# New priorities and engine homes in the list schedule of an attention and two expert layers

## The chip, the cores and the metric

The kernel runs on one core of one Trainium2 chip. The core has a matrix engine (TensorE, PE in the profile, with its weight loads as PEld), a vector engine (VectorE, DVE), a scalar engine (ScalarE, ACT), a general engine (GpSimd, POOL) and a queue that issues transfers (SyncE, SP). Each works off its own instructions in the order in which they were written and waits where a semaphore says so. The metric is the device time of one execution in microseconds, lower being better.

## The reference

```python
scores = scale * np.matmul(q, k.transpose(0, 1, 3, 2))       # 4 x 8 heads, 576 x 576, 64 wide
decay = cum[:, :, :, None] - cum[:, :, None, :]              # cum = cumsum(log(clip(f)))
scores = np.where(causal, -1e9, scores + decay)
attn = softmax(scores); x = attn @ v                         # to 2304 tokens x 512
h = x @ w_in1;  g = max(h, 0) + alpha * min(h, 0); x = g @ w_out1    # 512 -> 2048 -> 512
h = x @ w_in2;  g = h * tanh(softplus(h));         out = g @ w_out2  # 512 -> 2048 -> 512
```

The weights come in as 64-bit floats.

## The kernel before

**Attention.** The 32 heads are worked off as 16 pairs. For each pair: `load_qk`, `load_bias` and `load_v` bring the inputs; `stage_T` rounds q and k; `stage_M` computes the row maxima (TensorE, line 616, and a custom minimum on VectorE, line 623) and transposes them (line 635); `stage_S` computes the scores again with the maxima folded in (line 660), takes the exponential (ScalarE, line 670) and cuts the causal triangle (GpSimd, line 678); `stage_R` sums the weights on GpSimd (line 696) and TensorE (line 708, "the denominators" below) and inverts the sums; `stage_V` multiplies with v (line 742) and scales the result into X on VectorE (line 748).

**The first expert layer.** X is cut into six blocks of 384 tokens. A product of two 32-bit matrices is made of three matmuls of rounded values (high x high, low x high, high x low), so each operand is split: the high part is a cast on ScalarE (line 321), the low part a subtraction (line 331) on GpSimd or VectorE. The inner width of 2048 is cut into 16 slices. The first four slices of a block are `group_a` (stages A0 to A3 and B0 to B3): four groups of 12 matmuls (lines 786 to 788), the activation `prelu` (lines 805 to 814), the split of g, and 48 matmuls with the second weights (lines 851 to 853), whose four banks are copied out (line 321 on ScalarE or 323 on VectorE). Blocks 0 to 2 of `group_a` run inside the attention as a filler, blocks 3 to 5 behind it. Then `moe_block` works off the other twelve slices of all six blocks (stages H0 and O0). One such step is 24 matmuls.

**Weights.** A weight tile is loaded in two halves and converted to 32 bits by line 399 on ScalarE and 401, 403 and 405 on VectorE, then split. `w4_0` names the first matrix of slot 4, `w4_1` the second. There are two buffers for the conversion, wb0 and wb1; the second, and the slots 4 to 11, exist only once the attention has ended (`swap1`), since they take its memory. Twenty-four tiles are converted from then on for the first expert layer. The 32 tiles of the second layer are converted in the same way while the first runs, stored to memory and fetched later (`store_w`, `fetch_w`).

**The second expert layer** (lines 831 to 843 and 862 to 864) works like the first with another activation. It takes the time from about 650 us to the end.

**What sets the order.** Nothing is written out by hand. Every operation is given to a planner (`Plan.add`) with an engine, a cost from fixed formulas, a due time and the tiles that it reads and writes. `Plan.schedule` is a list scheduler: at each step it takes the engine that can start soonest and gives it the ready operation with the lowest priority number. `Plan.emit` runs it forwards and backwards ten times and writes the best order by its own costs. Two tables steer it. Both are looked up by the stage's name and the operation's number within the stage:

```python
at += PRIO.get(key[0], {}).get(key[1], 0.0)
if isinstance(eng, dict):
    alt, e = eng, ENG.get(key, next(iter(eng)))
    eng, cost, f = e, alt[e], fn
```

`PRIO` shifts the due time. `ENG` chooses the home of an operation that can run on more than one engine; without an entry it is the first that the call names. The planner knows that GpSimd and VectorE exclude each other in some operations (its `door`), and charges each of them its fixed cost.

Of the kernel before, what the change touches and what calls it, by code (L numbers as in the profile page):

```python
# [16 lines left out]

PRIO = {'': {0: -9.5, 1: -5.5, 2: -6, 3: -6.5, 4: -3.5}, 'A0': {0: -0.5, 1: -1, 2: 7.5, 3: 1.5}, 'A0g': {1: -13.5, 2: 0.5, 3: -8}, 'A1': {0: 50, 1: -24, 2: 1, 3: -44}, 'A1g': {0: -3.5, 1: 5, 2: 6, 3: -1}, 'A2': {0: 48.5, 2: -4, 3: 39.5}, 'A2g': {0: 2, 1: -7, 2: 10.5, 3: 5}, 'A3': {0: 9.5, 1: -8, 2: -30.5, 3: -28.5}, 'A3g': {0: 31, 1: 4, 2: 1, 3: -6}, 'AX': {1: 11.5, 2: 21.5, 3: -5, 4: 12, 5: 11.5, 6: 23.5, 7: 21}, 'B0': {0: -1.5, 1: -1.5, 2: 2, 3: 8, 4: -1}, 'B1': {0: -1.5, 1: -2, 2: -23, 4: -19.5}, 'B2': {0: 4.5, 1: 0.5, 2: -30.5, 3: 7.5, 4: 8.5}, 'B3': {0: -14.5, 1: 24, 2: -37.5, 3: 7, 4: 1.5, 5: -3.5}, 'H0': {0: -11, 1: -10.5, 2: -12.5, 3: -43, 4: -1, 5: 6.5, 6: 1.5}, 'H1': {0: -58, 1: -2.5, 2: -38.5, 3: -34.5, 4: -0.5, 5: 4, 6: 3, 7: 10, 8: -8, 10: 5.5, 11: -2, 12: 23, 13: -4.5, 14: -2}, 'O0': {0: 1, 1: -6.5, 2: -9.5, 3: -35, 4: -1, 5: 4.5, 6: 1.5, 7: 3.5}, 'O1': {0: -30.5, 1: 0.5, 2: -4.5, 3: 10.5, 4: -0.5, 5: 3, 6: 6.5, 7: 14.5, 8: 40.5}, 'W': {0: 14, 1: -4, 2: -12.5, 3: -7, 4: 34, 5: -23.5, 6: -12, 7: 9.5, 8: 30, 9: -6.5, 10: -30, 11: -5, 12: 1, 13: -29}, 'WA': {0: 2, 1: 0.5, 3: -25, 4: -10.5, 5: 6.5, 6: 2, 7: 5, 8: -41.5, 9: -9.5, 10: -6.5, 11: 4, 12: 5}, 'WF': {0: 9.5, 1: -8, 2: -58.5}, 'WS': {0: 4, 1: 8.5, 2: -17, 3: -53, 4: 1, 6: -0.5, 7: -1.5, 8: -15.5, 9: -23, 10: -12, 11: -28.5, 12: 3, 13: -2}, 'X0': {0: 3, 1: -22.5, 2: 45.5, 3: -5, 4: -2, 5: 11.5, 6: 16.5, 7: -14.5}, 'X1': {0: -10, 1: -1, 2: -4.5, 3: -22, 4: -4.5, 5: -5, 6: -22.5, 7: -13.5}, 'alph': {0: 14.5, 1: 13.5}}  # L20
ENG = {('A0g', 0): 'ACT', ('A1g', 0): 'ACT', ('A2g', 3): 'DVE', ('AX', 1): 'DVE', ('AX', 3): 'DVE', ('AX', 5): 'DVE', ('AX', 7): 'DVE', ('B3', 4): 'DVE', ('H0', 4): 'ACT', ('H1', 14): 'DVE', ('O1', 5): 'DVE', ('WF', 2): 'DVE', ('X0', 1): 'POOL', ('X0', 3): 'POOL', ('X0', 7): 'POOL', ('X1', 3): 'POOL', ('X1', 5): 'POOL', ('X1', 7): 'POOL'}


class Plan:
# [1017 lines left out]
```

## Time and profile before

| | |
|---|---|
| time, median of 3 runs | 1057.97 us (1057.28 to 1059.17) |
| profiled execution | 1058.0 us |
| its span, first to last instruction | 1056.2 us |
| TensorE busy | 1017.5 us, 96% |
| VectorE / ScalarE / GpSimd busy | 745.1 / 542.1 / 414.2 us |
| mean granted clock of TensorE | 0.994 |
| the attention's last matmul | at about 277 us |

Matmuls overlap, so a busy TensorE is read by its count of matmuls in a stretch beside the busy time. A wait is the idle time of an engine before an instruction, with the engine and line that ended it. The granted clock is a share of 2.4 GHz.

### The profile page before, as it was taken

How to read it: one execution, taken by the hardware profiler on the slowest of the kernel's cores; microseconds unless marked ns; L12 is line 12 of the kernel's file. 1: busy time of each engine (PE TensorE's matmuls, PEld its weight loads, DVE VectorE, ACT ScalarE, POOL GpSimd, SP SyncE). 2: the span in 40 equal slices, each digit the busy share in tenths (PEclk: the TensorE clock that was granted, in tenths of full speed). 3: DMA queues.
4: the chain of work that ended last, by engine and by line, in shares of the span. 5: the costliest groups of instructions: out<-in, count | busy, mean ns of one | idle time of the engine just before them, and what ended most of it. 6: DMA issues, size and time to landing. Idle time of an engine off the chain costs nothing.

```text
span 1056.2 us, 16992 instructions
## 1 busy us (share of the span) xinstructions
PE 1017.5 (96%) x5996; PEld 914.7 (87%) x5996; DVE 745.1 (71%) x1673; ACT 542.1 (51%) x1133; POOL 414.2 (39%) x423
## 2 busy tenths in 40 slices
...
PEclk9999999999999999999999999999999999999999
...
GB/s 163 89 110 98 79 70 36 71 48 12 44 117 100 125 137 183 183 207 182 163 1 1 20 92 129 41 1 31 1 6 25 1 30 1 1 31 1 31 1 31
DMA packets 55399, 71.06 MB, mean 67 GB/s; under 512 B 6673, under 2 KB 32273, under 8 KB 55313
## 3 DMA queue, kind: packets, MB, share of 16 engines
q1 hardware_dynamic: 55312, 69.97, 21.2%
...
## 4 chain that ended last, share of the span: by engine, by line
PE 85%; DVE 6%; DMA 3%; ACT 2%; issue 2%; POOL 1%; SPq 0%; ACTq 0%; DVEq 0%; POOLq 0%
PE b L786 12%; PE b L787 11%; PE b L788 11%; PE b L660 6%; PE b L863 6%; PE b L862 6%; PE b L864 6%; PE b L851 5%; PE b L853 5%; PE b L852 5%; PE b L742 4%; PE b L616 3%; PE b L519 2%; DVE wb L403 2%; PE b L708 2%
## 5 line engine op out<-in xcount | busy, mean ns | idle before, releaser
L786 PE MATMUL b<-xh,w 128*128 128x384 f32 x768 | 261.1, 340 | 9.0 <-ACT x L321 5.4
L788 PE MATMUL b<-xl,w 128*128 128x384 f32 x768 | 258.7, 337 | 0.0
L787 PE MATMUL b<-xh,w 128*128 128x384 f32 x768 | 258.6, 337 | 0.0
L843 POOL TENSOR_TENSOR x<-x 128x384 f32<-128x384 f32 x96 | 112.5, 1172 | 246.6 <-DVE x L841 165.7
L786 PEld LDWEIGHTS b<-xh,w 128*128 128x128 f32 x768 | 145.2, 189 | 17.6 <-ACT x L321 6.4
L787 PEld LDWEIGHTS b<-xh,w 128*128 128x128 f32 x768 | 145.2, 189 | 4.0
L788 PEld LDWEIGHTS b<-xl,w 128*128 128x128 f32 x768 | 145.0, 189 | 0.0
L331 POOL TENSOR_TENSOR g<-X,g 128x384 fp32r<-128x384 f32 x72 | 78.6, 1095 | 164.8 <-ACT g L321 128.4
L851 PE MATMUL b<-g,w 128*128 128x384 f32 x384 | 131.8, 343 | 9.4 <-DVE x L811 2.5
L853 PE MATMUL b<-g,w 128*128 128x384 f32 x384 | 129.8, 338 | 0.7 <-POOL g L331 0.6
L852 PE MATMUL b<-g,w 128*128 128x384 f32 x384 | 129.3, 337 | 0.0
L321 ACT CAST g<-x 128x384 fp32r<-128x384 f32 x120 | 61.4, 512 | 115.5 <-POOL x L843 105.0
L864 PE MATMUL b<-w,g 128*128 128x512 f32 x288 | 113.2, 393 | 0.0
L863 PE MATMUL b<-w,g 128*128 128x512 f32 x288 | 113.2, 393 | 0.0
L862 PE MATMUL b<-w,g 128*128 128x512 f32 x288 | 113.1, 393 | 0.0
L811 DVE SCALAR_TENSOR_TENSOR X<-X,alph,b 128x384 f32<-128x384 f32 x72 | 43.9, 611 | 84.3 <-ACT X L805 83.8
L623 DVE CUSTOM_DVE_ANT_0 junk<-b,tri 128x320 f32<-128x320 f32 (+3 forms) x160 | 69.4, 434 | 45.8 <-PE b L616 33.2
L331 DVE TENSOR_TENSOR g<-x,g 128x384 fp32r<-128x384 f32 x102 | 74.9, 736 | 17.6 <-ACT g L321 17.3
L399 ACT ACTIVATE wb<-raw 128x256 f32<-128x256 f32 x128 | 52.2, 432 | 66.8 <-DMA wd<-wb 38.2
L851 PEld LDWEIGHTS b<-g,w 128*128 128x128 f32 x384 | 72.6, 189 | 13.8 <-DVE x L814 3.4
L805 ACT ACTIVATE X<-b 128x384 f32<-128x384 f32 x72 | 35.2, 489 | 88.7 <-PE b L788 88.0
L401 DVE TENSOR_SCALAR wb<-wb 128x256 int32<-128x256 int32 x128 | 55.1, 450 | 33.9 <-ACT wb L399 33.0
...
## 6 DMA issues: line engine op xcount, KB each, us to landing
...
```

The source lines that it names most:

```text
L331: plan.add(engs, 0.0, at, lambda e: (nc.gpsimd if e == "POOL" else nc.vector).tensor_tensor(out=out(), in0=in0(), in1=in1(), op=ALU.subtra ...
L623: nc.vector.tensor_tensor_reduce(out=junk[ql, :z - a], in0=ps()[ql, :z - a], in1=tri[ql, x0 + a:x0 + z], scale=-1.0, scalar=BIG if n == 0 ...
L786: nc.tensor.matmul(ps[:, :NB], w[:, 0, c], xh[c], start=(c == 0), stop=False)
L787: nc.tensor.matmul(ps[:, :NB], w[:, 1, c], xh[c], start=False, stop=False)
L788: nc.tensor.matmul(ps[:, :NB], w[:, 0, c], xl[c], start=False, stop=(c == KC - 1))
L843: add("POOL", c_pool(NB, 2.2), lambda e, m: nc.gpsimd.tensor_tensor(out=m, in0=e, in1=m, op=ALU.mult), [ek, mk], [mk])
L851: nc.tensor.matmul(ps[:, :NB], w[:, 0, c], g[:, 0], start=first, stop=False)
L852: nc.tensor.matmul(ps[:, :NB], w[:, 1, c], g[:, 0], start=False, stop=False)
L853: nc.tensor.matmul(ps[:, :NB], w[:, 0, c], g[:, 1], start=False, stop=last)
L862: nc.tensor.matmul(ps, g[:, 0, sl], w[:, 0], start=first, stop=False)
L863: nc.tensor.matmul(ps, g[:, 0, sl], w[:, 1], start=False, stop=False)
L864: nc.tensor.matmul(ps, g[:, 1, sl], w[:, 0], start=False, stop=last)
```

## The change

Both tables get new numbers. `PRIO` had entries for stages of the expert layers and the weights; now it also has entries for the stages that the attention consists of (`LQ2`, `LB2`, `LV2`, `T2`, `M2`, `NM2`, `ST0` to `ST3`, `R2`, `pro2`), and nearly all others are changed. No other line of the kernel differs. The tables are one line each; here they are wrapped and cut.

```diff
-PRIO = {'': {0: -9.5, 1: -5.5, 2: -6, 3: -6.5, 4: -3.5}, 'A0': {0: -0.5, 1: -1, 2: 7.5, 3: 1.5},
...
+PRIO = {'': {0: -17.5, 1: -17.2, 2: -11, 3: -11.5, 4: -11.4}, 'A0': {0: -1.0, 1: -1, 2: 7.5, 3: -8.5},
...
+ 'LQ2': {0: -38.9, 1: 20}, 'LV2': {0: 6.3, 1: 20}, 'M2': {0: 20, 1: 6.1, 2: 20, 3: 27.7,
...
-ENG = {('A0g', 0): 'ACT', ('A1g', 0): 'ACT', ('A2g', 3): 'DVE', ('AX', 1): 'DVE', ('AX', 3): 'DVE',
- ('AX', 5): 'DVE', ('AX', 7): 'DVE', ('B3', 4): 'DVE', ('H0', 4): 'ACT', ('H1', 14): 'DVE',
- ('O1', 5): 'DVE', ('WF', 2): 'DVE',
...
+ENG = {('A0g', 0): 'ACT', ('A0g', 2): 'ACT', ('A0g', 3): 'POOL', ('A1g', 0): 'ACT', ('A2g', 2): 'ACT',
+ ('A2g', 3): 'DVE', ('A3g', 0): 'DVE', ('AX', 1): 'DVE', ('AX', 2): 'ACT', ('AX', 3): 'DVE',
+ ('AX', 4): 'ACT', ('AX', 5): 'DVE', ('AX', 7): 'DVE', ('B0', 4): 'DVE', ('B3', 4): 'DVE',
+ ('H0', 4): 'ACT', ('H0', 7): 'DVE', ('H1', 13): 'ACT', ('H1', 14): 'DVE', ('NM2', 1): 'ACT',
+ ('NM2', 2): 'ACT', ('O1', 3): 'DVE', ('O1', 5): 'ACT', ('R2', 3): 'POOL', ('T2', 2): 'ACT',
...
```

Many of the new homes name the engine that the operation had anyway. Of the program's instructions, 72 subtractions of line 331 move from GpSimd to VectorE (`('H0', 7)`), and 6 copies of a bank by line 321 on ScalarE become copies by line 323 on VectorE (`('B0', 4)`). In the second layer `('O1', 3)` and `('O1', 5)` exchange homes. Everything else is order.

What stands on TensorE at the end of the attention (b0 to b7 are banks; line 708 are the last pair's denominators, lines 786 to 788 the first matmuls of `group_a` for block 3, lines 851 to 853 the filler's second product), before:

```order
L742 MATMUL b5_70<-Pt1_123,vt1_146 64x64 x2
L708 MATMUL b0_65<-Pt1_123,ones_154 64x128 x2
L708 MATMUL b0_65<-accp_147,ones_154 64x160 x2
L708 MATMUL b1_66<-accp_147,ones_154 64x288 x2
L786 MATMUL b7_72<-xh0_96,w3_0_86 128x384
L787 MATMUL b7_72<-xh0_96,w3_0_86 128x384
```

And now:

```order
L708 MATMUL b0_65<-Pt1_123,ones_154 64x128 x2
L708 MATMUL b0_65<-accp_147,ones_154 64x160 x2
L708 MATMUL b1_66<-accp_147,ones_154 64x288 x2
L851 MATMUL b7_72<-g2_106,w2_1_85 128x384
L852 MATMUL b7_72<-g2_106,w2_1_85 128x384
L853 MATMUL b7_72<-g2_106,w2_1_85 128x384
L851 MATMUL b7_72<-g3_107,w3_1_87 128x384
L852 MATMUL b7_72<-g3_107,w3_1_87 128x384
L853 MATMUL b7_72<-g3_107,w3_1_87 128x384
L786 MATMUL b7_72<-xh0_96,w3_0_86 128x384
```

Six matmuls of the filler have moved behind the denominators.

What stands on ScalarE around the copy of bank b4, the first that block 3 of `group_a` frees (x2_3 is its result), before:

```order
L399 ACTIVATE wb0_92<-raw0_91 128x256 x2
L321 CAST w6_0_2651<-wb0_92 128x512
L399 ACTIVATE wb1_2643<-raw1_2642 128x256 x2
L399 ACTIVATE wb0_92<-raw0_91 128x256 x2
L321 COPY x2_3_2639<-b4_69 128x384
L321 CAST w5_1_2650<-wb1_2643 128x512
```

Now that copy stands on VectorE:

```order
L403 SCALAR_TENSOR_TENSOR wb1_2643<-raw1_2642,wb1_2643 128x256
L405 SCALAR_TENSOR_TENSOR wb1_2643<-raw1_2642,wb1_2643 128x256 x2
L331 TENSOR_TENSOR xl1_101<-X_111,xh1_97 128x384
L331 TENSOR_TENSOR xl2_102<-X_111,xh2_98 128x384
L323 COPY x2_3_2639<-b4_69 128x384
L331 TENSOR_TENSOR xl3_103<-X_111,xh3_99 128x384
```

and on ScalarE the copies of b5 and b6 come next:

```order
L399 ACTIVATE wb0_92<-raw0_91 128x256 x2
L805 ACTIVATE x2_4_2640<-b4_69 128x384
L399 ACTIVATE wb1_2643<-raw1_2642 128x256 x2
L321 COPY x2_3_2639<-b5_70 128x384
L321 CAST w6_0_2651<-wb0_92 128x512
L321 COPY x2_3_2639<-b6_71 128x384
```

The copy of b4 has left the queue in which conversions of line 399 stand, those of b5 and b6 have not.

What stands on VectorE in the main part of the first expert layer (four steps of the third block; line 811 is the activation, g0 to g3 the four buffers of its result), before:

```order
L811 SCALAR_TENSOR_TENSOR X_111<-X_111,alph1_75,b6_71 128x384
L905 TENSOR_TENSOR x2_1_116<-b2_67,x2_1_116 128x384
L401 TENSOR_SCALAR wb1_2643<-wb1_2643 128x256 x2
L403 SCALAR_TENSOR_TENSOR wb1_2643<-raw1_2642,wb1_2643 128x256 x2
L405 SCALAR_TENSOR_TENSOR wb1_2643<-raw1_2642,wb1_2643 128x256 x2
L811 SCALAR_TENSOR_TENSOR X_111<-X_111,alph1_75,b7_72 128x384
```

And now:

```order
L331 TENSOR_TENSOR g1_105<-X_111,g1_105 128x384
L811 SCALAR_TENSOR_TENSOR X_111<-X_111,alph1_75,b6_71 128x384
L401 TENSOR_SCALAR wb0_92<-wb0_92 128x256 x2
L403 SCALAR_TENSOR_TENSOR wb0_92<-raw0_91,wb0_92 128x256 x2
L331 TENSOR_TENSOR g2_106<-X_111,g2_106 128x384
L405 SCALAR_TENSOR_TENSOR wb0_92<-raw0_91,wb0_92 128x256 x2
L811 SCALAR_TENSOR_TENSOR X_111<-X_111,alph1_75,b7_72 128x384
```

The subtractions of g, which stood on GpSimd, now stand between the activations and the conversions.

## Rows read from the trace of the kernel before

**Rows 1.** The page: span, busy times, granted clock in 40 slices.

```profile
span 1056.2 us, 16992 instructions
...
PE 1017.5 (96%) x5996; PEld 914.7 (87%) x5996; DVE 745.1 (71%) x1673; ACT 542.1 (51%) x1133; POOL 414.2 (39%) x423
...
PEclk9999999999999999999999999999999999999999
```

**Rows 2.** Busy times by stretch: length, PE, PEld, DVE, ACT, POOL, clock, DMA, GB/s.

```profile
15.00:277.00 262.00, 250.45 (x1908) 190.54 (x1906) 160.59 (x565) 158.57 (x329) 131.59 (x161) 1.00 0.22 66
277.00:300.00 23.00, 16.10 (x88) 14.37 (x84) 18.05 (x42) 11.58 (x27) 10.80 (x7) 1.00 0.33 100
300.00:345.00 45.00, 40.04 (x204) 37.84 (x204) 38.61 (x78) 23.60 (x57) 21.96 (x18) 0.92 0.34 108
345.00:396.00 51.00, 50.99 (x294) 51.00 (x295) 35.84 (x84) 27.09 (x62) 31.85 (x26) 1.00 0.40 129
396.00:506.00 110.00, 106.53 (x602) 105.38 (x600) 89.62 (x194) 48.53 (x114) 33.27 (x32) 0.98 0.58 187
506.00:650.00 144.00, 142.82 (x824) 142.85 (x825) 54.51 (x96) 52.14 (x110) 47.67 (x44) 1.00 0.21 61
650.00:1045.00 395.00, 395.00 (x1997) 358.96 (x1996) 336.30 (x598) 210.41 (x422) 128.10 (x111) 1.00 0.05 17
```

**Rows 3.** TensorE's timeline: start, duration, instruction, [idle before, its releaser].

```profile
281.12 0.44 PE L786 MATMUL b<-xh,w 128*128 128x384 f32 x1 [1.45 <-DVE X L748]
...
288.72 0.45 PE L853 MATMUL b<-g,w 128*128 128x384 f32 x1 [0.64 <-POOL g L331]
...
291.56 0.44 PE L851 MATMUL b<-g,w 128*128 128x384 f32 x1 [1.33 <-DVE x L814]
...
300.58 0.69 PE L786 MATMUL b<-xh,w 128*128 128x384 f32 x1 [4.07 <-ACT x L321]
...
303.63 0.37 PE L786 MATMUL b<-xh,w 128*128 128x384 f32 x1
...
333.86 0.44 PE L851 MATMUL b<-g,w 128*128 128x384 f32 x1 [2.45 <-DVE x L811]
...
345.00 0.45 PE L786 MATMUL b<-xh,w 128*128 128x384 f32 x1 [1.32 <-ACT x L321]
...
402.12 0.41 PE L851 MATMUL b<-g,w 128*128 128x384 f32 x1 [2.21 <-ACT g L321]
```

**Rows 4.** GpSimd's timeline in the same form.

```profile
291.20 1.29 POOL L331 TENSOR_TENSOR w<-wb,w 128x512 fp32r<-128x512 f32 x1
295.86 3.53 POOL L331 TENSOR_TENSOR w<-wb,w 128x512 fp32r<-128x512 f32 x1 [3.37 <-ACT w L321]
...
329.10 2.09 POOL L331 TENSOR_TENSOR g<-x,g 128x384 fp32r<-128x384 f32 x2
...
393.37 1.76 POOL L331 TENSOR_TENSOR w<-wb,w 128x512 fp32r<-128x512 f32 x1 [2.43 <-ACT w L321]
```

**Rows 5.** ScalarE's timeline ahead of the wait that ended at 300.58.

```profile
299.42 0.75 ACT L399 ACTIVATE wb<-raw 128x256 f32<-128x256 f32 x2 [2.99 <-POOL w L331]
300.07 0.46 ACT L321 COPY x<-b 128x384 f32<-128x384 f32 x1
```

**Rows 6.** VectorE's timeline; the row at 294.36 is an undisturbed pair.

```profile
287.73 2.66 DVE L405 SCALAR_TENSOR_TENSOR wb<-raw,wb 128x256 int32<-128x256 int32 x2
...
294.36 0.75 DVE L405 SCALAR_TENSOR_TENSOR wb<-raw,wb 128x256 int32<-128x256 int32 x2
...
330.25 2.37 DVE L403 SCALAR_TENSOR_TENSOR wb<-raw,wb 128x256 int32<-128x256 int32 x2
...
337.94 0.54 DVE L331 TENSOR_TENSOR g<-x,g 128x384 fp32r<-128x384 f32 x1
```

**Rows 7.** Groups by line: count, busy us, mean ns, idle before and its releasers.

```profile
L331 POOL TENSOR_TENSOR g<-X,g 128x384 fp32r<-128x384 f32 x72 | 78.6, 1095 | 164.8 <-ACT g L321 128.4 <-DVE wb L401 19.8 <-PE b L853 10.0
L331 DVE TENSOR_TENSOR g<-x,g 128x384 fp32r<-128x384 f32 x102 | 74.9, 736 | 17.6 <-ACT g L321 17.3
...
L403 DVE SCALAR_TENSOR_TENSOR wb<-raw,wb 128x256 int32<-128x256 int32 x128 | 63.5, 524 | 0.3
```

More of the change, by code (lines that the diff above doesn't have):

```diff
@@ L16 @@
 PSUM = bass.MemoryType.PSUM
-PRIO = {'': {0: -9.5, 1: -5.5, 2: -6, 3: -6.5, 4: -3.5}, 'A0': {0: -0.5, 1: -1, 2: 7.5, 3: 1.5}, 'A0g': {1: -13.5, 2: 0.5, 3: -8}, 'A1': {0: 50, 1: -24, 2: 1, 3: -44}, 'A1g': {0: -3.5, 1: 5, 2: 6, 3: -1}, 'A2': {0: 48.5, 2: -4, 3: 39.5}, 'A2g': {0: 2, 1: -7, 2: 10.5, 3: 5}, 'A3': {0: 9.5, 1: -8, 2: -30.5, 3: -28.5}, 'A3g': {0: 31, 1: 4, 2: 1, 3: -6}, 'AX': {1: 11.5, 2: 21.5, 3: -5, 4: 12, 5: 11.5, 6: 23.5, 7: 21}, 'B0': {0: -1.5, 1: -1.5, 2: 2, 3: 8, 4: -1}, 'B1': {0: -1.5, 1: -2, 2: -23, 4: -19.5}, 'B2': {0: 4.5, 1: 0.5, 2: -30.5, 3: 7.5, 4: 8.5}, 'B3': {0: -14.5, 1: 24, 2: -37.5, 3: 7, 4: 1.5, 5: -3.5}, 'H0': {0: -11, 1: -10.5, 2: -12.5, 3: -43, 4: -1, 5: 6.5, 6: 1.5}, 'H1': {0: -58, 1: -2.5, 2: -38.5, 3: -34.5, 4: -0.5, 5: 4, 6: 3, 7: 10, 8: -8, 10: 5.5, 11: -2, 12: 23, 13: -4.5, 14: -2}, 'O0': {0: 1, 1: -6.5, 2: -9.5, 3: -35, 4: -1, 5: 4.5, 6: 1.5, 7: 3.5}, 'O1': {0: -30.5, 1: 0.5, 2: -4.5, 3: 10.5, 4: -0.5, 5: 3, 6: 6.5, 7: 14.5, 8: 40.5}, 'W': {0: 14, 1: -4, 2: -12.5, 3: -7, 4: 34, 5: -23.5, 6: -12, 7: 9.5, 8: 30, 9: -6.5, 10: -30, 11: -5, 12: 1, 13: -29}, 'WA': {0: 2, 1: 0.5, 3: -25, 4: -10.5, 5: 6.5, 6: 2, 7: 5, 8: -41.5, 9: -9.5, 10: -6.5, 11: 4, 12: 5}, 'WF': {0: 9.5, 1: -8, 2: -58.5}, 'WS': {0: 4, 1: 8.5, 2: -17, 3: -53, 4: 1, 6: -0.5, 7: -1.5, 8: -15.5, 9: -23, 10: -12, 11: -28.5, 12: 3, 13: -2}, 'X0': {0: 3, 1: -22.5, 2: 45.5, 3: -5, 4: -2, 5: 11.5, 6: 16.5, 7: -14.5}, 'X1': {0: -10, 1: -1, 2: -4.5, 3: -22, 4: -4.5, 5: -5, 6: -22.5, 7: -13.5}, 'alph': {0: 14.5, 1: 13.5}}
@@ L21 @@
-ENG = {('A0g', 0): 'ACT', ('A1g', 0): 'ACT', ('A2g', 3): 'DVE', ('AX', 1): 'DVE', ('AX', 3): 'DVE', ('AX', 5): 'DVE', ('AX', 7): 'DVE', ('B3', 4): 'DVE', ('H0', 4): 'ACT', ('H1', 14): 'DVE', ('O1', 5): 'DVE', ('WF', 2): 'DVE', ('X0', 1): 'POOL', ('X0', 3): 'POOL', ('X0', 7): 'POOL', ('X1', 3): 'POOL', ('X1', 5): 'POOL', ('X1', 7): 'POOL'}
+PRIO = {'': {0: -17.5, 1: -17.2, 2: -11, 3: -11.5, 4: -11.4}, 'A0': {0: -1.0, 1: -1, 2: 7.5, 3: -8.5}, 'A0g': {1: -13.5, 2: -16.5, 3: -21.1}, 'A1': {0: 50, 1: -24.7, 2: 1, 3: -42.4}, 'A1g': {0: -16.6, 1: 5, 2: 6, 3: -0.2}, 'A2': {0: 48.5, 2: -4, 3: 15.2}, 'A2g': {0: 12, 1: -22.0, 2: 30.6, 3: 15}, 'A3': {0: 9.5, 1: -8, 2: -42.3, 3: -28.5}, 'A3g': {0: 31, 1: 4, 2: 54.2, 3: -6}, 'AX': {1: 10.1, 2: 21.5, 3: -5, 4: 12, 5: 11.5, 6: 25.1, 7: 21}, 'B0': {0: 1.3, 1: -1.3, 2: 2, 3: 8, 4: -1}, 'B1': {0: 0.5, 2: -26.9, 3: 2, 4: -17.3}, 'B2': {0: 4.5, 1: 0.5, 2: -31.4, 3: 7.5, 4: 8.5}, 'B3': {0: -15.7, 1: 24, 2: -57.2, 3: 7, 4: 1.5, 5: -3.5, 6: 1.4, 7: 2.5}, 'H0': {0: -1, 1: -0.5, 2: -2.5, 3: -33, 4: 9, 5: 16.5, 6: 11.5, 7: 10}, 'H1': {0: -45.2, 1: -4.5, 2: -40.5, 3: -36.5, 4: -2.5, 5: 4.5, 6: 1, 7: 8, 8: -70.4, 9: -7.1, 10: 3.7, 11: -4, 12: -33.6, 13: -5.5, 14: -30.5}, 'LB2': {0: -1.6, 1: 2, 2: 2, 3: 2}, 'LQ2': {0: -38.9, 1: 20}, 'LV2': {0: 6.3, 1: 20}, 'M2': {0: 20, 1: 6.1, 2: 20, 3: 27.7, 4: 20, 5: 20, 6: 20, 7: -2.4, 8: 20, 9: 21.2, 10: 16.0, 11: 47.1, 12: 20, 13: 30.5, 14: 20, 15: 20, 16: 20, 17: 20, 18: 20, 19: 30.1, 20: 20, 21: 20.5, 22: 20, 23: 20.6}, 'NM2': {0: 0.6, 2: 4.6}, 'O0': {0: -1, 1: -8.5, 2: -11.1, 3: -37, 4: 29.1, 5: 2.5, 6: -0.5, 7: -0.1}, 'O1': {0: -8.5, 1: 22.5, 2: 17.4, 3: 41.2, 4: -9.7, 5: 25, 6: 15.8, 7: 36.5, 8: 62.5}, 'R2': {6: -0.3, 7: -4.9, 9: -1.8, 10: 3.8, 11: -25.5}, 'ST0': {1: 3.2, 3: -4.8}, 'ST1': {0: -6.4, 2: -1.6}, 'ST2': {2: -17.2}, 'ST3': {3: 53.3}, 'T2': {0: -5, 1: -5, 2: -5, 3: -5}, 'W': {0: 36.6, 1: -4, 2: -12.5, 3: -7.6, 4: 34, 5: -33.3, 6: -58.3, 7: 9.5, 8: 30, 9: -6.5, 10: -29.8, 11: -5, 12: 1, 13: -25.9}, 'WA': {0: 2, 1: 4.0, 3: -24.8, 4: -10.5, 5: 6.5, 6: 2, 7: 5, 8: -41.5, 9: -12.9, 10: -6.3, 11: 10.8, 12: 7.5}, 'WF': {0: 33.9, 1: 5.4, 2: -47.5}, 'WS': {0: 1, 1: 4.2, 2: -17, 3: -56, 4: -2, 5: -12.8, 6: -1.4, 7: -6.7, 8: -15.5, 9: -26, 10: -6.8, 11: -40.8, 13: -5.5}, 'X0': {0: -1.6, 1: -52.2, 2: 38.0, 3: -5, 4: -2, 5: 11.5, 6: 22.0, 7: -19.1}, 'X1': {0: -10.8, 1: -14.4, 2: -13.2, 3: -22, 4: -4.5, 5: 16.4, 6: -22.5, 7: -49.3}, 'alph': {0: 60.6, 1: 32.4}, 'const': {0: 46.5, 1: 2}, 'pro2': {1: -42.3, 3: -16.0, 7: -1.2, 8: -7.9, 11: 10.3, 12: 7.7, 13: 19.7, 18: -5.1, 21: -1.9, 22: 17.9, 24: -4.5, 25: 15.7, 26: -9.5, 27: 35.1}, 'warm2': {0: 6.0}}
```

1 line of the change is left out of this document (added).

## The prediction

> **What bounds the kernel now.** I read the page's first two parts first: TensorE is busy 1017.5 of 1056.2 us and its clock digits are all 9 [rows 1]. So the program is bound by TensorE, whose instructions the change only reorders, and all that can be won is time in which it waits or runs at the lower clock: 38.7 us in the whole span. The table of stretches shows where that lies [rows 2]. In the attention (15 to 277 us) TensorE lacks 11.55 us of 262, in 277 to 300 it lacks 6.90, in 300 to 345 it lacks 4.96, in 396 to 506 it lacks 3.47, in 506 to 650 it lacks 1.18, and from 650 to 1045 nothing. The rest is the first 7 us and the tail, where the order hardly changes. In a stretch without waits, 345 to 396, 294 matmuls take 50.99 us: 0.1734 us each, which I use below as the price of one.
>
> The third view is TensorE's own timeline with its waits [rows 3]. Seven waits stand between the last attention matmul and 403 us: 1.45, 0.64, 1.33, 4.07, 2.45, 1.32 and 2.21 us, together 13.5 us. Three of them cost twice: after the 4.07 us wait the next nine matmuls take 3.05 us (300.58 to 303.63) where 9 x 0.1734 = 1.56 would do, so 1.5 us goes to the clock; the mean granted clock of 300 to 345 is 0.92, that of 396 to 506 is 0.98, all others 1.00 [rows 2], so the waits of 2.45 and 2.21 have such a stretch at 1.2 GHz too. With 3 x 1.5 the handover from attention to the first expert layer loses 18.0 us. That is where I look for the gain; the attention's 11.55 us lie in some twenty short waits.
>
> The fourth view is what the other engines did at those moments. At 300.58 TensorE waited for ScalarE's copy of bank b4. That copy ended at 300.53 but stood behind a conversion of line 399 that waited 2.99 us for GpSimd [rows 5], and GpSimd was in one subtraction of a weight tile for 3.53 us, where the one before took 1.29 [rows 4]. At 333.86 it waited for line 811 on VectorE, which stood behind two conversions that took 2.37 us instead of 0.75 while GpSimd ran two subtractions in 2.09 us [rows 4, 6]. So these two engines stretch each other, and an order planned with fixed costs breaks there. The Trainium skill says the same (SBUF — State Buffer, Who interferes with whom): a VectorE instruction with two SBUF inputs and a GpSimd one that reads SBUF exclude each other for the whole instruction. The trace agrees, with the four numbers above.
>
> **The change part by part.** Of all the new homes only two change a program: 72 subtractions of line 331 (the low parts of g in the first expert layer's main blocks) go from GpSimd to VectorE, and 6 bank copies (B0) from ScalarE to VectorE. All else is order.
>
> (a) End of attention. TensorE waited 1.45 us at 281.12 for the last scaling of X on VectorE, which hangs on the denominators (line 708). Before, 12 matmuls stood between the denominators and the waiting one; now 18. 6 x 0.1734 = 1.04 us of cover: -1.0. Bounds -1.45 (it goes) and +1 (the denominators themselves come later).
>
> (b) The waits of 0.64 (GpSimd, g) and 1.33 (line 814). ScalarE and GpSimd no longer do a weight tile between two g's (a GpSimd weight subtraction is 1.29 us, so the 0.64 goes), and lines 807 and 814 of the third group stand behind 8 conversions instead of 12. The last two before them took 2.66 us [rows 6]; a pair without disturbance takes 0.75, so 1.0 of the 1.33 goes even if one pair stays stretched. Together -1.6, bounds -1.97 and +1.
>
> (c) The 4.07 us wait. The copy that frees b4 is now on VectorE between subtractions of xl, and waits for no GpSimd instruction. Thirty matmuls later TensorE wants b5, whose copy is still on ScalarE behind two such conversions. I count what GpSimd's stretch costs there (3.53 - 1.29 = 2.2 us) as left: -(4.07 + 1.5 - 2.2) = -3.4. Bounds -5.6 and 0.
>
> (d) The waits of 2.45, 1.32 and 2.21 with two slow stretches: 9.0 us. The first goes by order: line 811 of b5 now follows that of b4 directly. But the second matrices of each weight pair are converted later: the last one, w3_1, ends its conversion 25 VectorE rows later, at about 0.5 us (a mean of 0.52 for line 403, [rows 7]) some 12.5 us. Before, its conversion and subtraction ended at 395.1 [rows 4], and its first use came 300 matmuls after the row at 345.00, so at 397.0: 1.9 us of slack. Now its first use comes 369 matmuls after that place, 12.0 us later, but TensorE arrives there about 8 us sooner by (a) to (d). 1.9 + 12.0 - 12.5 - 8 = -6.6: it would wait 6.6 us, with one slow stretch of 1.5. Net -(9.0 - 6.6 - 1.5) = -0.9. The bounds are -9.0 (the supply keeps up: 12 lows less on GpSimd per block of 50 us free it for 12 x (1.10 - 0.54) = 6.7 us of the pair's shared time, [rows 6, 7]) and +6.6.
>
> (e) Attention. The table now holds numbers for the stages that make up the attention, so its order changes everywhere after the first pairs, but no instruction moves to another engine. The last attention matmul stands at place 1352 of 5392 instead of 1358, and changes between the three kinds of matmul before it number 132 instead of 134. Of the 11.55 us of short waits some will go and others come. I take 0, bounds -6 and +6 (half of them gone, or half as many again).
>
> (f) The 72 subtractions on VectorE. Free of GpSimd they cost 0.54 us (the row at 337.94), on GpSimd 1.05 (2.09 for two) to 1.10 [rows 4, 7]. What hides them is VectorE's slack: in 345 to 396 it is busy 35.84 of 51, in 396 to 506 89.62 of 110, in 506 to 650 54.51 of 144 [rows 2]. A step of 24 matmuls takes 4.16 us, so 26 fall into the 110 us: 26 x 0.54 = 14 us, or 103.7 of 110. That fits, so 0, with -3.5 (the waits of that stretch go) and +16 (below) as bounds.
>
> From 650 us on TensorE has no gap to lose or win, and the last three copies and stores stand as before but for their engines: 0.
>
> Sum: -1.0 - 1.6 - 3.4 - 0.9 + 0 + 0 = -6.9. The profiled execution took 1058.0 us for its span of 1056.2; the median of the runs is 1057.97. So 1051.
>
> **Rivals.**
> Larger gain: the supply keeps up and the short waits of the attention halve. Terms (a) to (d) at their lower bounds give 18.0 and (e) 6, so -24 at most; halfway between that and the forecast lies 1042. For it speaks that GpSimd has less to do in the blocks after the handover; against it, that waits of 0.2 to 1 us have other reasons in every order.
>
> No net change: the waits are moved, not removed. The planner counts fixed costs and the stretches to 3.53 and 2.37 us are outside them, so a new order meets new ones. (c) and (d) at 0, one of the gains in (a) and (b) spent: 1057.
>
> Slower, one mechanism: VectorE becomes the bound of the first expert layer between 345 and 506 us. It converts the second layer's weights there, and each group of four g's now has its low parts in the same queue, each behind conversions and behind ScalarE's cast. At the mean of a VectorE subtraction in the trace (0.736, [rows 7]) the 26 add 19.1 us, which with 89.6 makes 108.7 of 110: from about 105 of 110 on TensorE waits for g. At 3 us of waits for each of four blocks and three slow stretches of 1.5 us that is +16.5, less the 6.9: 1068. For it speaks VectorE's load, against it that GpSimd's lows no longer stretch the conversions. The Trainium skill bears on this (Perfetto Trace Analysis, Optimizing Scalar/DVE Operations): a saturated VectorE may shed work, but to GpSimd it may not help since they share a port. By its first half this move would be a loss here, by its second hardly one; the rows at hand speak more for the second.
>
> **How the numbers follow.** Forecast (1046 to 1055): 0.46. Larger gain (below 1046): 0.17. No net change, within 0.2% or 2.1 us of 1058, which is about what a measurement can tell: 0.14. Slower: 0.23, since (e) can turn against me as well. Faster is 0.46 + 0.17 = 0.63. The range takes in most of the larger gain and the lower half of the slower case: 1041 to 1064. The forecast's own range is 1046 to 1055.
>
> **What would show it.** (a): the wait for line 748 at the first expert group is under 0.6 us. (b), (c): TensorE waits less than 3 us in the 25 us after the last attention matmul, and no stretch at the lower clock follows. (d): a wait for a weight tile's second matrix or its conversion about 100 us after the attention's end. (e): TensorE lacks 8 to 14 us before the last attention matmul. (f): VectorE is busy under 95% in the first expert layer, and no wait of TensorE there names a VectorE subtraction of g. The prediction is wrong if the attention's end moves by more than 6 us, or if TensorE waits more than 5 us for g between 350 and 600.

## The result: 1031.2 us instead of 1057.6

The changed kernel takes 1031.16 us (median of 4 runs, 1031.08 to 1032.97) beside 1057.62 us of the kernel before on the same chip: a ratio of 0.9753, with a 95% interval of 0.9736 to 0.977. The forecast was 1051, in a range from 1041 to 1064. So the sign was right and the size was wrong: -26.5 us measured, -6.9 predicted. One profiled execution among those below, that of experiment 2, took 2004 us with matmuls of 557 ns instead of about 337, and none of its rows are read.

The page after, beside [rows 1]:

```profile
span 1029.4 us, 16893 instructions
...
PE 1009.9 (98%) x5996; PEld 909.7 (88%) x5996; DVE 746.0 (72%) x1751; ACT 537.7 (52%) x1127; POOL 336.7 (33%) x351
...
PEclk9999999999999999999999999999999999999999
```

The span is 26.8 us shorter. TensorE's idle time fell from 38.7 us to 19.5 (1029.4 - 1009.9), which is 19.2 of it; the other 7.6 is its busy time, 1017.5 before. The matmuls are the same 5996, so they ran at a better pace. About 4.5 us of it, by the prediction's own estimate, are the three stretches at 1.2 GHz, which are gone. Most of the rest goes with the waits. The matmul ahead of a wait is not overlapped by the next one (0.34 us instead of 0.17), and the one behind it takes longer to the next start (0.28 us at 281.12 before); summed over the starts of all matmuls this is about 11.5 us before and 8.8 after. VectorE, with 78 operations more, is busy no longer than before (746.0 against 745.1), and GpSimd, with 72 less, 77.5 us less.

The stretches after, in the order of [rows 2], and one more row for 15 to 270 us (length, PE, PEld, DVE, ACT, POOL, clock, DMA, GB/s):

```profile
15.00:270.00 255.00, 250.02 (x1915) 190.07 (x1913) 155.47 (x564) 155.27 (x327) 130.62 (x161) 1.00 0.22 69
...
15.00:277.00 262.00, 256.31 (x1950) 196.06 (x1949) 161.14 (x578) 158.47 (x334) 132.92 (x163) 1.00 0.22 68
277.00:300.00 23.00, 21.43 (x120) 20.37 (x119) 20.45 (x40) 13.12 (x31) 11.03 (x9) 1.00 0.29 93
300.00:345.00 45.00, 43.58 (x249) 43.06 (x250) 39.75 (x89) 23.35 (x53) 22.05 (x16) 1.00 0.37 116
345.00:396.00 51.00, 50.99 (x295) 50.67 (x293) 44.87 (x105) 26.85 (x62) 16.99 (x12) 1.00 0.42 134
396.00:506.00 110.00, 109.89 (x631) 109.06 (x631) 87.92 (x229) 49.27 (x117) 6.58 (x6) 1.00 0.63 202
506.00:650.00 144.00, 144.00 (x824) 142.86 (x823) 78.48 (x140) 62.53 (x126) 15.83 (x14) 1.00 0.21 59
```

TensorE has done by 270 us (250.02) what it had done by 277 before (250.45 in [rows 2]): in waits the attention gives 6.6 us. Its end moves by more, 8.6 us, of which 1.0 are the six matmuls that now stand behind it. The denominators' last group, before and then after:

```profile
276.44 0.93 PE L708 MATMUL b<-accp,ones 128*64 128x160 f32 x8
```

```profile
267.84 0.93 PE L708 MATMUL b<-accp,ones 128*64 128x160 f32 x8
```

From 277 to 345 TensorE lacks 1.57 + 1.42 = 3.0 us instead of 11.9, at the full clock (a wait of 0.72 us now falls ahead of 277), and from 396 to 650 it lacks 0.1 us instead of 4.7. Its waits behind the attention are now these (in the form of [rows 3]), and one of 0.28 us at 321.42; behind that none is left:

```profile
270.75 0.44 PE L786 MATMUL b<-xh,w 128*128 128x384 f32 x1 [0.72 <-DVE x L323]
...
280.27 0.44 PE L853 MATMUL b<-g,w 128*128 128x384 f32 x1 [0.34 <-POOL g L331]
...
286.65 0.44 PE L786 MATMUL b<-xh,w 128*128 128x384 f32 x1 [1.19 <-DVE x L323]
...
301.15 0.44 PE L851 MATMUL b<-g,w 128*128 128x384 f32 x1 [1.20 <-DVE x L814]
```

That is 3.7 us where [rows 3] had 13.5 and three slow stretches. The last weight tile's subtraction on GpSimd, which ended at 395.1 before [rows 4], is this row after:

```profile
386.10 1.42 POOL L331 TENSOR_TENSOR w<-wb,w 128x512 fp32r<-128x512 f32 x1 [3.83 <-ACT w L321]
```

It ends at 387.5, 7.6 us earlier, but the attention ends 8.6 us earlier too. Counted from there the tile is 1.0 us later, where I had counted 12.5. VectorE's share of that way, before and then after (columns as in [rows 2]):

```profile
277.00:395.10 118.10, 106.23 (x581) 102.30 (x578) 92.50 (x202) 62.26 (x144) 63.72 (x51) 0.97 0.36 114
```

```profile
268.40:387.50 119.10, 115.38 (x655) 112.60 (x652) 102.80 (x224) 65.07 (x150) 52.35 (x39) 1.00 0.36 112
```

VectorE does 22 operations and 10.3 us of work more in it and takes 1.0 us longer.

### The profile page after: what moved, and what is told of

Its sections match the earlier page's. It is cut to its first block, busy times and chain, and to the rows that moved or that the text cites. A ratio compares the mean times of both kernels' runs of the same rounds, so it can differ in the third digit from the quotient of the medians.

```text
span 1029.4 us, 16893 instructions
## 1 busy us (share of the span) xinstructions
PE 1009.9 (98%) x5996; PEld 909.7 (88%) x5996; DVE 746.0 (72%) x1751; ACT 537.7 (52%) x1127; POOL 336.7 (33%) x351
## 4 chain that ended last, share of the span: by engine, by line
PE 91%; DVE 5%; issue 1%; POOL 1%; ACT 1%; DMA 0%; DVEq 0%; POOLq 0%; ACTq 0%
PE b L786 13%; PE b L787 12%; PE b L788 12%; PE b L864 6%; PE b L863 6%; PE b L862 6%; PE b L851 6%; PE b L853 6%; PE b L660 6%; PE b L852 6%; PE b L742 4%; PE b L616 3%; PE b L519 2%; PE b L708 2%; DVE junk L623 1%
## 5 line engine op out<-in xcount | busy, mean ns | idle before, releaser
L786 PE MATMUL b<-xh,w 128*128 128x384 f32 x768 | 259.0, 337 | 2.3 <-DVE x L323 2.1
L786 PEld LDWEIGHTS b<-xh,w 128*128 128x128 f32 x768 | 144.2, 188 | 8.7 <-DVE x L323 3.0
L331 DVE TENSOR_TENSOR g<-x,g 128x384 fp32r<-128x384 f32 x102 | 71.9, 707 | 38.2 <-ACT g L321 37.6
L331 POOL TENSOR_TENSOR xl<-X,xh 128x384 fp32r<-128x384 f32 x18 | 19.4, 1087 | 174.1 <-ACT xh L321 126.8
L851 PEld LDWEIGHTS b<-g,w 128*128 128x128 f32 x384 | 72.1, 188 | 4.3 <-DVE x L814 1.8
L670 ACT ACTIVATE Pt<-b 128x288 f32<-128x288 f32 (+1 forms) x128 | 56.4, 502 | 37.2 <-PE b L660 36.7
L853 PEld LDWEIGHTS b<-g,w 128*128 128x128 f32 x384 | 72.1, 188 | 1.9 <-DVE g L331 1.3
```

Of the source, the lines that this page charges most:

```text
L331: plan.add(engs, 0.0, at, lambda e: (nc.gpsimd if e == "POOL" else nc.vector).tensor_tensor(out=out(), in0=in0(), in1=in1(), op=ALU.subtra ...
L786: nc.tensor.matmul(ps[:, :NB], w[:, 0, c], xh[c], start=(c == 0), stop=False)
L851: nc.tensor.matmul(ps[:, :NB], w[:, 0, c], g[:, 0], start=first, stop=False)
L853: nc.tensor.matmul(ps[:, :NB], w[:, 0, c], g[:, 1], start=False, stop=last)
```

## The experiments

One kernel holds both tables, plans both orders (the operations have the same numbers in both), and picks at emission from which plan each operation is taken and, where HOMES says so, on which engine it runs:

```diff
+TABLES = {'before': (PRIO_before, ENG_before), 'after': (PRIO_after, ENG_after)}
...
+                both[t] = (e, eng[e], a, lambda e=e, f=fn: f(HOMES.get(key, e)))
...
+        made = {t: self.plan(t) for t in TABLES}
+        for n, t in mixed(made["before"][0], made["after"][0], self.keys):
+            made[t][2][n][3]()
```

So an order can be cut and spliced, and a home changed without a new plan. The lines of these kernels are 21 to 47 higher than those of after; each fence below says by how many. The ratios stand against the kernel before on the same chip; after itself is at 0.9753. Spans are those of the profiled executions, 1056.2 before and 1029.4 after.

**1. After, lows on GpSimd.** `HOMES = {('H0', 7): 'POOL'}`, the order of after.

> The order of after, word for word, but the 72 low halves of g in the first expert layer (H0, entry 7) are run by GpSimd again. Theory 1, the order carries the gain: the attention (-6.5 us) and the handover (-13.2 us) lie before or barely in these 72, so at most the 6.3 us won between 395 and 510 us come back: 1031 to 1038 us, forecast 1035. Theory 2, the homes carry it (GpSimd's lows stretch VectorE's conversions, and that starved TensorE): the waits for weights and x of 300 to 510 us return, 1045 us or more, and conversions of 512 columns take longer from 320 us on.

1036.7 us, ratio 0.9822 (0.9797 to 0.9848), span 1034.9: 5.5 us of span come back, all behind 325 us. TensorE's waits from 325 to 510 us, where after has none (lines 21 higher; waiter, releaser, us in total, times, longest):

```profile
PE b L874 <- POOL g L352: 1.9, 4, 0.7
PE b L873 <- POOL w L352: 0.7, 1, 0.7
PE b L808 <- POOL w L352: 0.7, 1, 0.7
PE b L872 <- ACT g L342: 0.4, 1, 0.4
```

Weights and g's both come late from GpSimd, in which they stand in one queue. And VectorE's conversions in that stretch take longer. First this kernel, then after (count, busy us, mean ns, idle before):

```profile
L426 DVE SCALAR_TENSOR_TENSOR wb<-raw,wb 128x256 int32<-128x256 int32 x90 | 45.9, 531 | 0.5
L424 DVE SCALAR_TENSOR_TENSOR wb<-raw,wb 128x256 int32<-128x256 int32 x90 | 45.5, 521 | 0.6
L422 DVE TENSOR_SCALAR wb<-wb 128x256 int32<-128x256 int32 x91 | 38.0, 429 | 23.9 <-ACT wb L420 23.7
```

```profile
L403 DVE SCALAR_TENSOR_TENSOR wb<-raw,wb 128x256 int32<-128x256 int32 x92 | 40.4, 455 | 0.8 <-DVE wb L401 0.2
L405 DVE SCALAR_TENSOR_TENSOR wb<-raw,wb 128x256 int32<-128x256 int32 x92 | 38.5, 439 | 0.3
L401 DVE TENSOR_SCALAR wb<-wb 128x256 int32<-128x256 int32 x91 | 29.2, 331 | 15.6 <-ACT wb L399 15.2
...
L331 DVE TENSOR_TENSOR g<-X,g 128x384 fp32r<-128x384 f32 x44 | 26.7, 610 | 3.2 <-ACT g L321 3.1
```

With the lows on GpSimd the conversions cost VectorE 129.4 us, without them 108.1: 21.3 us less, which pays for most of the 26.7 us of the 44 lows that VectorE takes over in that stretch. The Trainium skill (SBUF — State Buffer, Who interferes with whom) lets a VectorE instruction with two SBUF inputs and a GpSimd read exclude each other; the means of 455 against 521 ns and 439 against 531 ns agree. The third group, of one input, is not covered by that sentence and gets shorter as well, 331 against 429 ns.

**2. Before, lows on VectorE.** `HOMES = {('H0', 7): 'DVE'}`, the order of before.

> The order of before, word for word, but the 72 low halves of g are run by VectorE, at the places that they had. Theory 1, the order carries the gain: the four waits of the handover stay, and of the 6.3 us between 395 and 510 us a part goes: 1052 to 1058 us, forecast 1054. Theory 2, the homes carry it: 1040 us or less. Third possibility: 72 more operations on VectorE at the places planned for GpSimd delay its conversions, 1058 to 1070 us.

1053.2 us, ratio 0.9969 (0.9955 to 0.9983): 3.3 us, as forecast.

**3 and 4. The attention exchanged.** SWAP1 are the three operations that close the attention; number 4 has before and after exchanged.

```diff
+    for t, last in (("before", SWAP1), ("after", ("H0", 0)), ("after", None)):
+        o = orders[t]
+        end = len(o) if last is None else max(o.index(x) for x in last) + 1 if last is SWAP1 else next(i for i, n in enumerate(o) if keys[n] == last)
+        out += [(n, t) for n in o[:end] if n not in done]
+        done.update(o[:end])
```

> The order of before up to the operation that hands the attention's memory over (all of the attention and what is interleaved with it), from there on the order and homes of after. If the gains of the stages add: the 6.5 us of the attention are lost and all else is kept, 1037.5 us (1036 to 1039). Rival, the later waits vanished because the attention ended sooner: 1045 us or more. Rival, a later attention costs nothing since TensorE then waits less: 1031 to 1033 us.

> The counterpart: the order of after up to the handover of the attention's memory, from there on the order and homes of before. If the gains add: 1057.6 - 6.5 = 1051 us (1050 to 1053). Rival, the handover of before is bound by VectorE's and GpSimd's work, which does not end sooner, so its waits grow by what the attention wins: 1057 us, with about 6 us more waiting between 270 and 400 us.

Number 3: 1041.3 us, ratio 0.9858 (0.9841 to 0.9876), span 1039.4, 10.0 us longer than after's, more than the 6.5 forecast. The 1.45 us wait for X is back in front of the first L786. In the profiled execution some 2.2 us more are a stretch at the lower clock inside the attention:

```profile
96.00:100.00 4.00, 3.99 (x21) 2.77 (x23) 1.46 (x8) 3.84 (x9) 2.55 (x3) 0.57 0.12 34
```

Two other executions have a mean granted clock of 1.00 and take as long (1041.53 and 1041.95 us), so for them these 2 us stay open. Number 4: 1050.25 us, ratio 0.994 (0.9918 to 0.9963), span 1049.3, 6.9 us under before's. So the attention's gain stands by itself; the waits of before follow some 8 us earlier.

**5 and 6. The six bank copies.** `HOMES = {('B0', 4): 'ACT'}` in the order of after, `'DVE'` in that of before.

> The order of after, but the six copies that empty the bank of the first output chunk of a token block (B0, entry 4) run on ScalarE again, as in before. The first matmul of the next block waits for this copy (L786: 4.07 and 1.32 us before, 0.72 and 1.19 after). If the home carries the handover's gain, a wait of 2 us or more returns in front of L786 and the time is 1034 us or more; if the order carries it, the copy finds ScalarE free and the time stays within 1.5 us of after, 1030 to 1032.5 us. Forecast 1032.

> The order of before, but the same six copies run on VectorE. If ScalarE's queue (the copy stood behind a cast that waited 2.99 us for GpSimd) made the 4.07 us wait, it falls to about 1 us, with it the 1.5 us of the slower clock behind it, and the 1.32 us falls a little: 1057 - 4.5 = 1052.5 us (1051 to 1054). If VectorE is as late there, or the next wait takes the gain, 1056 to 1058 us.

Number 5: 1031.43 us, ratio 0.9748 (0.9733 to 0.9763): the same as after. Number 6: 1055.14 us, ratio 0.9976 (0.9965 to 0.9987), span 1052.6. The 4.07 us wait fell to 1.22 as expected, but only 2.5 us of the 4.5 reached the end. In the profiled execution a stretch at 1.2 GHz now stands behind the 1.34 us wait at 292.91 (1.33 us at 291.56 before, without one), so the clock's 1.5 us are not saved. This home is a cure for a bad order and worth nothing in a good one.

**7 and 8. After until the first expert layer, then before.** The splice of number 3 with ("after", SWAP1), ("after", ("H0", 0)), ("before", None); number 8 also has `HOMES = {('H0', 7): 'DVE'}`.

> The order of after up to the first operation of the first expert layer's second part (H0), from there the order and homes of before (72 lows on GpSimd). If the stages add, the attention (6.5) and the handover (13) stay won and the 6 to 7 us won after 325 us are lost: 1037 us (1036 to 1039), the same as after's order with these lows on GpSimd, so the order behind this point is worth nothing by itself. Rival, the order of the conversions behind this point matters too: 1041 us or more.

> The same, with the 72 lows on VectorE and nothing else changed against the run before. If the homes of the lows carry what is won after 325 us: 1031 to 1033 us, and the mean of VectorE's conversions falls as in after. If the order of the rest carries it: 1037 us, no change against the run before. If lows at places planned for GpSimd come too late on VectorE: between, 1033 to 1036 us, with waits of TensorE for g.

1051.96 us, ratio 0.9944 (0.9929 to 0.9959), and 1048.69 us, ratio 0.9907 (0.989 to 0.9924). My theory had 1037 and 1031 to 1033. The miss is one wait at the seam, 12.11 us (12.41 in number 8) in front of the first matmul of an H0 group, for a copy of a bank on ScalarE. After leaves 37 operations of the weight conversion for later than before does; in before's order they come first thing, and the copy stands behind them. This is what sent me to the next two.

**9 and 10. Only these 37 moved.** TensorE's sequence is untouched. In number 9 (`base` is after's order, `other` before's) they stand behind the operations that they follow in before's order, or as soon behind as their inputs allow; number 10 is the reverse.

```diff
+    for n in other:
+        e = ops[n][0]
+        if n in MOVED:
+            rank[n] = max(rank[last[e]] + 1e-3, cut)
+        last[e] = n
```

> The order of after, with TensorE's sequence untouched; only the 37 operations of the weight conversion that before has ahead of the first expert layer's start and after has behind it (loads, casts, bit operations and lows of the fourth and fifth weight pairs) stand again behind the operations that they follow in before. Theory: these conversions, standing in VectorE's, ScalarE's and GpSimd's queues ahead of what TensorE needs next, made the handover's waits. Then 6 to 13 us come back: 1037 to 1044 us, forecast 1040, with single waits of 2 us or more between 285 and 345 us. Rival: the handover's gain comes from the order of the output chunks and of x on the engines, and these conversions matter little: 1030 to 1033 us.

> The counterpart: the order of before, with TensorE's sequence untouched, and these 37 operations moved behind the operations that they follow in after. Theory: 6 to 13 us of the handover's 13.2 are won without any other change: 1045 to 1052 us, forecast 1049. Rival: nothing is won, 1056 us or more, or less than is lost later, since VectorE then converts later with its conversions still lengthened by GpSimd: waits for weights behind 345 us.

Number 9: 1049.65 us, ratio 0.9943 (0.9927 to 0.996). Of the 18 us, 11.93 are one wait, and 1.46 one more. ScalarE ahead of the long one, which ends at 339.33 us (lines 47 higher: L368 is line 321, L446 line 399):

```profile
331.52 0.43 ACT L446 ACTIVATE wb<-raw 128x256 f32<-128x256 f32 x1 [1.62 <-DMA raw<-in_moe_w_out_dram]
...
334.10 0.62 ACT L368 CAST w<-wb 128x512 fp32r<-128x512 f32 x1 [1.55 <-DVE wb L452]
...
338.29 0.62 ACT L368 CAST w<-wb 128x512 fp32r<-128x512 f32 x1 [2.91 <-DVE wb L452]
338.81 0.47 ACT L368 COPY x<-b 128x384 f32<-128x384 f32 x1
```

The copy's bank had been ready since about 326 us. In the 12 us from 326.83 on ScalarE works some 4 us and else waits: for the load, then for VectorE's bits, then for the next load. What stands behind a conversion in a queue waits for its whole way over the engines.

Number 10: 1074.91 us, ratio 1.018 (1.0158 to 1.0201). My theory had 1049; deferring alone is a loss of 18 us. Up to 345 us the theory holds: the matmul that before starts at 345.00 starts at 338.80. The loss comes behind it. TensorE there (lines 47 higher):

```profile
354.58 0.69 PE L898 MATMUL b<-g,w 128*128 128x384 f32 x1 [5.22 <-ACT g L368]
387.30 0.69 PE L833 MATMUL b<-xh,w 128*128 128x384 f32 x1 [9.40 <-ACT w L368]
```

Here the weight supply does fall short, as step (d) had it, though in before's order and not in after's. So when conversions run is not the point by itself; each must stand where neither the operand behind it nor its own weight is needed before it is through.

**11 and 12. Which entries win the attention.** Up to SWAP1 the order comes from a third plan, behind it from after. ATT are the 14 entries of the attention's stages and constants.

```diff
+TABLES["mixed"] = ({k: v for k, v in P_A.items() if k not in ATT}, TABLES["after"][1])   # 11
+TABLES["mixed"] = ({**P_B, **{k: P_A[k] for k in ATT if k in P_A}}, TABLES["before"][1])  # 12
```

> Up to the attention's last operation the order comes from a plan with after's table without the 14 entries of the attention's stages and constants; from there the order of after. If these entries carry the attention's gain: the attention ends about 6 us later and the time is that of the run with the attention of before, 1038 to 1042 us. If the entries of the expert layer's work inside the attention (A0 to B3, AX, WA) carry it: 1030 to 1033 us.

> Up to the attention's last operation the order comes from a plan with before's table and these 14 entries of after added; from there the order of after. If these entries carry the attention's gain: 1030 to 1034 us. If the entries of the expert layer's work inside the attention carry it, or the two only fit together: 1038 to 1042 us.

1037.89 us, ratio 0.984 (0.9809 to 0.9871), and 1040.3 us, ratio 0.9853 (0.9838 to 0.9867). Their spans are 1035.8 and 1037.9, beside 1029.4 of after and 1039.4 of number 3: alone neither half wins more than 3.6 us of the 10. By TensorE's waits in the attention, though, each half wins: 11.5 us before (10.4 to 11.5 in the other runs with its attention), 8.2 in number 11, 8.7 in number 12, 5.0 after. Number 12 loses its part again to the clock, with stretches at 1.2 GHz at 70 to 77 and 281.6 to 285 us, some 5 us by the starts of their matmuls; all four of its executions have a mean granted clock of 0.994 to 0.995. Number 11, at the full clock, is 6.4 us of span behind after, of which 3.9 are idle time of TensorE; the rest is not put down to rows. The first of the two stretches:

```profile
70.00:77.00 7.00, 6.94 (x30) 5.31 (x30) 3.33 (x16) 3.94 (x8) 3.38 (x4) 0.51 0.24 74
```

From 40 to 160 us TensorE waits in after as the first fence shows, and in number 11 as the second (lines 31 higher: L647 is line 616, L654 line 623):

```profile
PE b L616 <- DVE M L623: 1.0, 3, 0.4
PE b L616 <- DVE nmx L623: 0.5, 2, 0.3
```

```profile
PE b L647 <- DVE M L654: 2.2, 6, 0.5
PE b L647 <- DVE nmx L654: 1.7, 3, 1.2
```

The waits are for M and nmx, which VectorE makes. Most of the entries for stage M are +20, so that it comes later in the plan; number 12 has these entries and not the filler's new places. Over the whole attention the waits for M and nmx are 6.0 us before (4.9 to 5.9 in the other runs with its attention), 5.9 in number 11, 4.9 in number 12 and 4.0 after. So with the filler's new places the entries take 1.9 us off these waits; with the old ones it is not clear, and that they do it by the later place is argued, not shown. The waits of the filler's own matmuls are 2.6 us before, 2.4 in number 12, 0.7 in number 11 and 0.6 after: they go with the filler's new places.

**13. Two copies three places later.** The order of after; on ScalarE the copies of the second and third bank of the last block before H0 stand behind two first steps of a conversion and one cast.

```diff
+    copies = [1642, 1647]
+    o = [n for n in base if n not in copies]
+    i = o.index(1807) + 1
+    rest = o[cut:i] + copies + o[i:]
```

> The order of after with two operations of ScalarE moved and nothing else: the copies that empty the second and third bank of the last block's output chunks (324.50 and 325.00 us in after) stand three places later on ScalarE, behind two first steps of a conversion and one cast of a weight (which ended at 327.8). TensorE reaches the second of these banks at about 325.9 us. If what a place behind a conversion costs is the conversion's whole way over the engines and not its busy time: TensorE waits 2.4 us or more there, with the slower clock behind it if such a wait brings one, 1033.5 to 1036 us. If only the busy time of the three (about 1.4 us) counts and TensorE has other work: 1031 to 1032 us.

1034.99 us, ratio 0.9795 (0.9775 to 0.9814), span 1032.0: two of 1127 ScalarE operations, three places, 2.6 us of span. TensorE, then ScalarE (lines 44 higher: L365 is line 321, L443 line 399):

```profile
328.40 0.44 PE L830 MATMUL b<-xh,w 128*128 128x384 f32 x1 [2.15 <-ACT x L365]
```

```profile
325.47 1.00 ACT L443 ACTIVATE wb<-raw 128x256 f32<-128x256 f32 x2 [1.08 <-DMA raw<-in_moe_w_out_dram]
327.35 0.62 ACT L365 CAST w<-wb 128x512 fp32r<-128x512 f32 x1 [0.87 <-DVE wb L449]
327.87 0.85 ACT L365 COPY x<-b 128x384 f32<-128x384 f32 x2
```

In after ScalarE reaches the two copies 0.29 us ahead of their bank and starts them at 324.50. Here they start 3.4 us later, though the work put ahead of them is only 1.6 us: the rest is its waits for a load and for VectorE. The Trainium skill (PSUM — Partial Sum Buffer, Engine vs sequencer instructions) calls ScalarE's queue strictly first in, first out; the ready copy behind a waiting cast agrees.

**14. The stretch between, of before.** The splice of number 3 with ("after", SWAP1), ("before", ("H0", 0)), ("after", None).

> The order of after up to the attention's last operation, then that of before up to the first operation of H0, then after's order and homes to the end. If the handover's gain sits in the stretch between (before has 37 conversion operations more in it): waits as in before come back, 4.07 us in front of L786 and one more, 1038 to 1044 us, forecast 1040. If it sits in what stands behind H0's start: 1031 to 1034 us.

1041.58 us, ratio 0.9854 (0.9837 to 0.9871), span 1038.5: 9.1 us of span, in this stretch and just behind it. TensorE's waits and the row of 270 to 300 us (lines 28 higher):

```profile
291.98 0.69 PE L814 MATMUL b<-xh,w 128*128 128x384 f32 x1 [4.57 <-ACT x L349]
...
325.38 0.45 PE L879 MATMUL b<-g,w 128*128 128x384 f32 x1 [2.44 <-DVE x L839]
```

```profile
270.00:300.00 30.00, 23.80 (x117) 22.44 (x118) 23.38 (x53) 13.87 (x34) 15.36 (x10) 0.89 0.28 91
```

The waits of 4.07 and 2.45 us in [rows 3] are back, and the lower clock with the first of them.

**15. Before with all homes.** `HOMES = {('H0', 7): 'DVE', ('B0', 4): 'DVE'}`, the order of before.

> The order of before with all homes of after that matter, the 72 lows and the six copies on VectorE. Alone they won 3.3 us and 2.5 us. If the two add: 1051 us (1049.5 to 1052.5), and the rest of the gain, 20 us, is the order's alone. If they share a cause: 1053 to 1055 us. If the homes are what the late conversions needed, no more than these 5.8 us are to be had here, since the order is before's.

1050.8 us, ratio 0.9944 (0.9925 to 0.9963): as forecast, the two homes add.

**16. Number 10 with the lows on VectorE.** `HOMES = {('H0', 7): 'DVE'}`.

> The run that moved 37 conversion operations behind in before's order (1074.9 us, with waits of 5.2 and 9.4 us for ScalarE's casts at 354 and 387 us), now with the 72 lows on VectorE. If the weights came late because GpSimd was full and VectorE's conversions were lengthened by it: most of the 18 us is won back, 1055 to 1062 us. If they came late because ScalarE's and VectorE's queues have something else ahead of them: 1070 us or more, less only the 3 us that these homes are worth anyway.

1070.93 us, ratio 1.0133 (1.0115 to 1.0152): 4 us less than number 10, and the waits of 5.36 and 7.17 us stay. The late weights there are the work of the queues, not of a full GpSimd.

**The sum.** Each part of before put back alone into after costs span: the lows' home 5.5 us (1), the stretch between 9.1 us (14), the attention 10.0 us (3). That is 24.6 of 26.8, so the parts nearly add. Put alone into before, the attention wins 6.9 us of span (4); all homes win 5.7 us by the medians (15). The orders of the attention and of what follows it are each worth more than the homes. Which of these two is larger is not settled: 10.0 against 9.1 put back into after, 6.9 against a remainder of some 14, which no run tests alone, put into before.

## Why the prediction was wrong, step by step

(a) held: the wait for line 748 is gone, and 0.72 us for a bank copy stands there. (b) held: 0.34 us is left of 1.97.

(c) was right in direction and too small: 1.19 us and no slow stretch are left of 4.07 + 1.5, a gain of 4.4 us for the 3.4 forecast. The reason given was half right. The copy's new home removes that wait in before's order (6), but in after's it makes no difference (5): the order of the stretch does it (14). That it is the place of the copies ahead of conversions is shown for two other copies (13).

(d) is the step that failed. I let the weight supply eat 8.1 of the 9.0 us; all three waits are gone, and only 1.20 us (0.24 before) and 0.28 us stand in their stretch now. I turned 25 rows more in VectorE's queue into 12.5 us of delay; measured from the attention's end it is 1.0 us. That queue was not full: from there to the last tile VectorE was busy 92.50 of 118.1 us, and is busy 102.80 of 119.1 now. The rows went into its waits. TensorE did arrive sooner, as I had it, and yet the slack held: 1.9 us in my count, 2.1 after (the tile ends at 387.5, and the matmul that I counted as its first use starts at 389.59). Experiment 10 shows that the danger was real: there the work that before does from 345.0 to 395.2 us takes 74.3 us instead of 50.2; what I lacked was a walk through ScalarE's queue with its waits.

(e) failed on size: 0 forecast with bounds of 6, 6.6 measured. I argued that as many short waits would come as go, since the counts of switches (132 and 134) and the last matmul's place barely moved. Neither count says how long TensorE waits. Of the 6.6 us, 2.0 are waits for M and nmx, 2.0 the waits of the filler's matmuls, 1.0 waits for X and 1.2 one wait without a releaser in the profile; the rest is small. Experiments 11 and 12 show that the table's new entries for these stages, which were in the diff, and the filler's new places each win a part of it.

(f) was right that VectorE takes the 72 lows, and wrong to price that at 0: by experiment 1 they win 5.5 us in after's order, beyond the bound of -3.5. In before's order they win 3.3 (2), in the mixed ones 3.3 (8 against 7) and 4.0 (16 against 10). I had taken GpSimd's stretch of VectorE into account for single rows [rows 4, 6] and not for the sum: 21.3 us of conversions in 185 us. The slower rival fails on the same number. VectorE stands at 87.92 of 110 us from 396 to 506 where I had 103.7 and the rival 108.7. The half of the Trainium skill's rule that I trusted (Perfetto Trace Analysis, Optimizing Scalar/DVE Operations: the two share a port, so work given to GpSimd may not help) is borne out by experiment 1.

Among the rivals the larger gain was the right one, with 0.17. Its price, 24 us at most, left out the lower bound of (f). Of these 3.5 us, 2.2 are the wait at 402 that (d) already counts, so with the rest it would have been 25.3, still short of the 26.5. Of the marks set for it, two were hit: the attention's end moved by more than 6 us, and no second matrix was waited for.

The frame was too narrow as well: the 38.7 us that I called all that can be won is idle time alone. The lower clock, and the matmuls beside a wait, stand in the busy time, and 7.6 of the 26.8 us came from there.

What stays open: some 2 us of number 3 in the executions at the full clock, and what the order behind the attention is worth alone in before's.
